# Moving output projections, product order and vector sums in three groups of a fused attention and MLP kernel

## Chip, cores, metric

One core of a Trainium2 chip. The metric is the device time of one execution in microseconds (us); the median over executions is quoted with its range. The profiler's span of an execution is some 1.8 us shorter than its time.

## The reference, cut to what matters

```python
x = A_x                                            # 1 x 2048 x 576, bf16
h = x + A(layernorm(x), A_wqkv, A_wo)              # dilated sliding-window attention, then "@ wo"
h2 = h + B(layernorm(h), B_w1, B_b1, B_w2, B_b2)   # MLP: gelu(y @ w1 + b1) @ w2 + b2, hidden width 4608
```

## The kernel before

The 16 tiles of 128 tokens are done in eight groups of two. A group has MLP1 (its results in PSUM go through gelu on ScalarE), the output projection `@ wo` of the next group's two tiles, LayerNorm of those, and MLP2. So a group's projections start the chain that ends with the next group's normalized, transposed rows.

From group 3 on, MLP2 multiplies part of its 18 pairs of row blocks in 2x2 blocks with seven products instead of eight. Each "product" n is a run of matmuls that add into one PSUM bank, and their left and right sides are partly sums made by VectorE. Pairs beyond `rows` (8, 12, 12, 16, 18, 18 in groups 3 to 8) are done in the plain way. One product's result starts several outputs: ScalarE copies it ("seeds") from one bank into another, `b` from the first product's bank into the sixth's, `d` from the sixth's into the fifth's, `f` from the fifth's into the third's.

```python
bank = {1: a, 2: a, 3: f, 4: b, 6: b}          # 7 and 5: banks of the projections' PSUM tiles, free after "h"
seed = {"b": (1, 6), "d": (6, 5), "f": (5, 3)}
if SR < rows < NM:        # group 6
    steps = [(1, all_), "b", "wo", "h", "e", (2, all_), "11", (6, lo), (7, lo), "6", "7", (6, hi), "d", (7, hi), "rest", "in",
             (5, all_), "f", "exp", (4, all_), "21", "22", "o1", "4", (3, all_), "12", "o0", "3"]
elif rows <= SR:          # groups 3 to 5
    steps = [(1, all_), "b", "wo", "h", "e", (2, all_), "11", (6, all_), "d", "6", "7", (7, all_), "rest", "in", ...]
elif not last:            # group 7
    steps = [(1, lo), "wo", (1, hi), "b", "h", "e", (7, lo), (6, all_), "d", "6", "7", (2, all_), (7, hi), "rest", "in", ...]
...                       # cut: group 8
```

An entry like `(6, lo)` is product 6 over the first 12 pairs of row blocks (`hi`: the rest, `all_`: both), "wo" the projections, "11" and its like plain rows. "h", "6", "7", "in" are hooks: what VectorE, ScalarE and the queues get at that point of their own orders. In "h" are the residual adds (`ln2_h`, which read the projections' PSUM tiles and so free them), LayerNorm's statistics (`ln2_act`, ScalarE) and sums for the products; in "6" and "7" LayerNorm's applies (`ln2_send`).

```python
def ln2_h(j):                                   # residual add on VectorE
    pw = pw_of.pop(j)
    h = sb.tile([P, D], F32, tag="h", name="h", bufs=2)
    nc.vector.tensor_tensor(out=h[:]..., in0=pw[:, :, 0:HALF], in1=x_of(j)..., op=ALU.add)

def phase(duo, swap, after):                    # MLP1 and the projections: pairs of 64-row matmuls
    ... nc.tensor.matmul(duo["g"][r ^ swap][i], lhsT=lhsT, rhs=rhs, ...)   # lhsT, rhs: 64 partitions
```

## Time and profile before

| | us |
|---|---|
| median of the first three runs | 365.69 (365.05 to 365.73) |
| span of the profiled run | 363.3 |
| group 5, MLP1's end to MLP2's end | 18.69 |
| group 6 | 18.65 |
| group 7 | 17.96 |

TensorE's order is fixed, so the stretch from the end of a group's last MLP1 matmul to the end of its last MLP2 matmul, read from TensorE's timeline, repeats within 0.02 us where nothing waits. Whole executions scatter by half a microsecond or more.

The following line is of TensorE's timeline (start, length, engine, line, operation, count), just before the wait for the seed copy that the prediction shows at 283.34.

```profile
282.65 0.41 PE L667 MATMUL po<-w2b_sb,h_all 128*128 128x288 f16 x2
```

Two matmuls are recorded with 0.41 us, 0.286 for the last, but matmuls follow each other every 0.1226. The next could have started at 282.65 + 2 x 0.1226 = 282.90, and it started at 283.34. So 0.44 us is lost. Lost time is read from starts.

### The profile page before, as it was taken

How to read it: one execution, taken by the hardware profiler on the slowest of the kernel's cores; microseconds unless marked ns; L12 is line 12 of the kernel's file. 1: busy time of each engine (PE TensorE's matmuls, PEld its weight loads, DVE VectorE, ACT ScalarE, POOL GpSimd, SP SyncE). 2: the span in 40 equal slices, each digit the busy share in tenths (PEclk: the TensorE clock that was granted, in tenths of full speed). 3: DMA queues.
4: the chain of work that ended last, by engine and by line, in shares of the span. 5: the costliest groups of instructions: out<-in, count | busy, mean ns of one | idle time of the engine just before them, and what ended most of it. 6: DMA issues, size and time to landing. Idle time of an engine off the chain costs nothing.

```text
span 363.3 us, 11427 instructions
## 1 busy us (share of the span) xinstructions
PE 357.6 (98%) x4895; PEld 290.5 (80%) x4895; DVE 300.6 (83%) x426; ACT 228.9 (63%) x507; POOL 39.4 (11%) x47
## 2 busy tenths in 40 slices
PE   8999999999999999999999999999999999999996
PEld 4688877888788877887788778877887788778874
DVE  5999999999999999999999899979998498720431
ACT  4779856799526763668556855685568656615630
POOL 2251004000120030103100211020101010100000
PEclk9999999999999999999999999999999999999999
DMA  7989899964445733720552145304530352030001
GB/s 235 299 204 306 223 260 236 363 219 78 145 89 107 218 111 87 152 40 34 137 106 71 35 125 115 72 32 109 118 71 33 74 102 56 3 89 19 2 2 33
DMA packets 61908, 43.70 MB, mean 120 GB/s; under 512 B 31889, under 2 KB 60177, under 8 KB 61857
## 3 DMA queue, kind: packets, MB, share of 16 engines
q1 hardware_dynamic: 59968, 41.13, 41.1%
q0 software_dynamic: 1728, 1.77, 4.8%
q8 instruction: 38, 0.62, 0.7%
q10 hardware_dynamic: 160, 0.07, 0.1%
q14 instruction: 14, 0.11, 0.1%
HBM read 21.10 MB, written 12.42 MB: 92 GB/s over the span
## 4 chain that ended last, share of the span: by engine, by line
PE 94%; DMA 2%; ACT 1%; SPq 1%; DVE 0%; issue 0%
PE pm L217 39%; PE po L667 25%; PE pq L217 14%; PE po L579 10%; PE pw L217 5%; DMA wq_sb<-in_A_wqkv_dram 1%; SPq L104 1%; PE xt_pt L182 1%; DMA x_all<-b_bc 1%; ACT hn L175 0%; ACT hn L479 0%; PE h_pt L182 0%; PE o_pt L182 0%; DVE h L461 0%; ACT hn L478 0%
## 5 line engine op out<-in xcount | busy, mean ns | idle before, releaser
L560 ACT ACTIVATE h_all<-pm,b_sb 128x256 f16<-128x256 f32 (+1 forms) x288 | 108.3, 496 | 74.3 <-PE pm L217 74.3
L217 PE MATMUL pm<-hnT,w_sb 64*128 64x256 bf16 x2304 | 143.0, 269 | 0.0
L217 PEld LDWEIGHTS <-w_sb 64*128 64x128 bf16 x2304 | 111.6, 94 | 15.1 <-issue 1.7
L667 PEld LDWEIGHTS <-h_all 128*128 128x128 f16 x528 | 50.8, 98 | 14.9 <-issue 2.5
L217 PE MATMUL pq<-wq_sb,xnT 64*128 64x288 bf16 x768 | 54.5, 283 | 0.8 <-DMA wq_sb<-in_A_wqkv_dram 0.7
L217 PEld LDWEIGHTS <-xnT 64*128 64x128 bf16 x864 | 42.4, 94 | 11.3 <-issue 1.1
L351 DVE TENSOR_TENSOR prod<-prod 128x2304 bf16<-128x2304 bf16 (+1 forms) x64 | 44.2, 691 | 2.1
L667 PE MATMUL po<-w2a_sb,h_all 128*128 128x288 bf16 (+1 forms) x302 | 42.0, 286 | 0.0
L397 DVE TENSOR_TENSOR prod<-kv_ring,probs 128x4608 bf16<-128x4608 bf16 x16 | 40.9, 2554 | 0.8 <-DMA kv_ring<-kv_dram 0.5
L345 DVE TENSOR_TENSOR prod<-kv_ring,q_all 128x4608 bf16<-128x4608 bf16 x16 | 40.8, 2549 | 0.2
L217 PE MATMUL pm<-hnT,w1h_sb 64*128 64x256 bf16 x288 | 39.2, 269 | 0.0
L403 DVE TENSOR_TENSOR prod<-prod 128x2304 bf16<-128x2304 bf16 (+1 forms) x32 | 33.8, 1057 | 1.0
L579 PEld LDWEIGHTS <-h_all 128*128 128x128 bf16 x288 | 27.8, 98 | 7.9 <-issue 1.0
L481 POOL TENSOR_TENSOR ln_rstd<-ln_var,mhalf 128x1 f32<-128x1 f32 x13 | 14.5, 1115 | 175.1 <-ACT ln_var L480 175.1
L667 PEld LDWEIGHTS <-kv_ring 128*128 128x128 f16 x240 | 23.5, 98 | 6.4 <-issue 0.5
L579 PE MATMUL po<-w2a_sb,h_all 128*128 128x288 bf16 x224 | 28.5, 286 | 0.0
L647 DVE TENSOR_TENSOR kv_ring<-h_all 128x1536 f16<-128x1536 f16 (+3 forms) x10 | 6.9, 687 | 17.3 <-ACT h_all L560 17.3
L667 PE MATMUL po<-w2b_sb,h_all 128*128 128x288 bf16 (+1 forms) x142 | 21.2, 286 | 0.0
L217 PE MATMUL pw<-wo_sb,oT 64*128 64x288 bf16 x256 | 19.5, 283 | 0.0
L162 POOL TENSOR_TENSOR ln_rstd<-ln_veps,mhalf 128x1 f32<-128x1 f32 (+2 forms) x14 | 13.3, 954 | 48.2 <-DVE ln_veps L156 31.8
L217 PEld LDWEIGHTS <-oT 64*128 64x128 bf16 x288 | 13.5, 94 | 4.8 <-issue 1.7
L739 ACT COPY po<-po 128x288 f32<-128x288 f32 x18 | 6.9, 384 | 16.2 <-PE po L667 13.0
(117 smaller groups left out, 383.1 us busy)
## 6 DMA issues: line engine op xcount, KB each, us to landing
w_sb<-in_B_w_dram SPq DMA_DIRECT2D x6, 768.0 KB, 5.5
kv_ring<-kv_dram SPq DMA_DIRECT2D x28, 144.0 KB, 2.6
w2a_sb<-in_B_w_dram SPq DMA_DIRECT2D x4, 1008.0 KB, 6.6
kv_dram<-kv_ring SPq DMA_DIRECT2D x13, 288.0 KB, 3.3
out_dram<-o_sb SPq DMA_DIRECT2D x15, 144.0 KB, 2.5
td<-q_all SPq DMA_DIRECT2D x14, 144.0 KB, 2.2
td<-hn SPq DMA_DIRECT2D x14, 144.0 KB, 1.8
x_all<-in_A_x_dram SPq DMA_DIRECT2D x12, 144.0 KB, 2.9
```

The lines of the kernel that those rows point to most:

```text
L162: nc.gpsimd.tensor_tensor(out=rstd[:], in0=veps[:], in1=mhalf[:].to_broadcast([P, n]), op=ALU.pow)
L217: last = nc.tensor.matmul(duo["g"][r ^ swap][i], lhsT=lhsT, rhs=rhs, start=(swap == 0 and i == 0 and kt == 0), stop=(swap == 1 and kt == K ...
L345: nc.vector.tensor_tensor(out=prod[:], in0=k_ring[j % 2], in1=q_all[:, j, :].unsqueeze(1) .to_broadcast([P, W, D]), op=ALU.mult)
L351: nc.vector.tensor_tensor(out=prod[:, :, o * H:o * H + n], in0=prod[:, :, a * H:a * H + n], in1=prod[:, :, c * H:c * H + n], op=ALU.add)
L397: nc.vector.tensor_tensor(out=prod[:].rearrange("p w (d h) -> p w d h", h=H), in0=v_ring[j % 2].rearrange("p w (d h) -> p w d h", h=H), in ...
L403: nc.vector.tensor_tensor(out=prod[:, 0:n, :], in0=prod[:, 0:n, :], in1=prod[:, n:2 * n, :], op=ALU.add)
L481: nc.gpsimd.tensor_tensor(out=rstd[:], in0=var[:], in1=mhalf[:], op=ALU.pow)
L560: pace[0] = nc.scalar.activation(out=hT(grp)[:, f, 0:N], in_=ps[:, r, i * N:(i + 1) * N], func=ACT.Gelu_apprx_tanh, bias=b1_sb[:, f:f + 1] ...
L579: nc.tensor.matmul(banks[half], lhsT=hT(grp)[:, f, i * P:(i + 1) * P], rhs=w2_rows(f)[:, half * HALF:(half + 1) * HALF], start=(f == 0), s ...
L647: nc.vector.tensor_tensor(out=s_slot(t, m0, m1), in0=a, in1=b, op=alu)
L667: nc.tensor.matmul(bank, lhsT=l, rhs=r, start=start, stop=stop, skip_group_check=True)
L739: nc.scalar.copy(out=bank[seed[step][1]], in_=bank[seed[step][0]])
```

## The change

In groups 5 to 7 the projections are issued first, directly behind MLP1; in groups 5 and 6 the seventh product's first rows come between the first and second product (in group 7 they lay there already), and plain rows (in 6 also the seventh product's last rows) lie between the sixth and the fifth, which waits for the sixth's seed copy. The first residual add and LayerNorm's first statistics get a hook of their own ("hc") ahead of the first seed copy. In group 6 the seventh product's sum, and in group 7 the sums of rows 12 to 17, go behind the residual adds. The intent is a TensorE without gaps. Cut to its core:

```diff
-        if SR < rows < NM:
-            steps = [(1, all_), "b", "wo", "h", "e", (2, all_), "11", (6, lo), (7, lo), "6", "7", (6, hi), "d", (7, hi), "rest", "in",
-        ...
+        if rows < NM:
+            steps = [(1, all_), "b", "wo", "hc", "h", "e", (2, all_), "11", (6, all_), "d", "6", "7", (7, all_), "rest"] if not first_wo \
+                else ["wo", "hc", (1, all_), "b", "h", "e", (7, lo), (2, all_), (6, all_), "6", "d", "rest", "7", "11"] if rows == SR \
+                else ["wo", "hc", (1, all_), "b", "h", "e", (7, lo), (2, all_), (6, all_), "6", "7", "d", "11", (7, hi), "rest"]
+            steps += ["in", (5, all_), "f", "exp", (4, all_), "21", "22", "o1", "4", (3, all_), "12", "o0", "3"]
         elif not last:
-            steps = [(1, lo), "wo", (1, hi), "b", "h", "e", (7, lo), (6, all_), "d", "6", "7", (2, all_), (7, hi), "rest", "in",
+            steps = ["wo", "hc", (1, all_), "b", "h", "e", (7, lo), (6, all_), "6", "d", "7", (2, all_), (7, hi), "rest", "in",
 ...
-                early = {2: (), 3: (0,)}.get(k, (0, 2))
+                early = {2: (), 4: (0, 2)}.get(k, (0,))
 ...
+                if k == 5:                                             # k counts groups from 0
+                    x["h"] += [c_(h_sums, 0, SR, (2,)), c_(h_sums, 0, SR, (1, 3))]
 ...                                                                    # group 7: sums of rows 12 to 17 behind the adds
-                    x["h"] = [c_(ln2_stats, c, d)] + x["h"]
+                    x["hc"] = [c_(ln2_h, c), c_(ln2_act, c)] + x["hc"]
+                    x["h"] = [c_(ln2_h, d), c_(ln2_act, d), c_(put_b2, c), c_(put_b2, d)] + x["h"]
 ...
-            mlp2_fast(g, rows, (p, q, r, s), wo, x)
-            p, q, r, s = r, s, p, q
+            if 4 <= k < 7:
+                mlp2_fast(g, rows, (s, p, q, r), wo, x, True)          # other PSUM tiles for the projections
+                p, q, r, s = q, r, p, s
+            else:
+                mlp2_fast(g, rows, (q, p, r, s), wo, x)
+                p, q, r, s = r, s, p, q
```

More of the change, by code (lines that the diff above doesn't have):

```diff
@@ L683, in halves, with mlp2_fast @@
         return ap.rearrange("p (g c) -> p g c", g=2)
-    def mlp2_fast(g, rows, tags, wo, hooks):
-        p, q, r, s = tags
+    def mlp2_fast(g, rows, tags, wo, hooks, first_wo=False):
         last = wo is None
+        q, p, r, s = tags
         j0, j1 = g
@@ L722, in mlp2_fast @@
         }
-        if SR < rows < NM:
-            steps = [(1, all_), "b", "wo", "h", "e", (2, all_), "11", (6, lo), (7, lo), "6", "7", (6, hi), "d", (7, hi), "rest", "in",
-                     (5, all_), "f", "exp", (4, all_), "21", "22", "o1", "4", (3, all_), "12", "o0", "3"]
-        elif rows <= SR:
-            steps = [(1, all_), "b", "wo", "h", "e", (2, all_), "11", (6, all_), "d", "6", "7", (7, all_), "rest", "in",
-                     (5, all_), "f", "exp", (4, all_), "21", "22", "o1", "4", (3, all_), "12", "o0", "3"]
+        if rows < NM:
[3 more added lines that the diff above has]
+            steps += ["in", (5, all_), "f", "exp", (4, all_), "21", "22", "o1", "4", (3, all_), "12", "o0", "3"]
         elif not last:
-            steps = [(1, lo), "wo", (1, hi), "b", "h", "e", (7, lo), (6, all_), "d", "6", "7", (2, all_), (7, hi), "rest", "in",
+            steps = ["wo", "hc", (1, all_), "b", "h", "e", (7, lo), (6, all_), "6", "d", "7", (2, all_), (7, hi), "rest", "in",
                      (5, all_), "f", (4, all_), "o1", (3, all_), "o0"]
@@ L1015 @@
             home = k % 2
-            x = {n: [] for n in ("h", "6", "7", "in", "exp", "4", "3")}
+            x = {n: [] for n in ("hc", "h", "6", "7", "in", "exp", "4", "3")}
             if k < 6:
@@ L1025 @@
                     m1[3] += [c_(w2_sums, 0, 8)]
-                early = {2: (), 3: (0,)}.get(k, (0, 2))
+                early = {2: (), 4: (0, 2)}.get(k, (0,))
                 m1[3] += [c_(h_sums, 0, min(rows, SR), early)]
-                x["h"] += [c_(h_sums, 0, min(rows, SR), [t for t in range(4) if t not in early])]
+                if k == 5:
+                    x["h"] += [c_(h_sums, 0, SR, (2,)), c_(h_sums, 0, SR, (1, 3))]
+                else:
+                    x["h"] += [c_(h_sums, 0, rows, [t for t in range(4) if t not in early])]
                 if k == 5:
@@ L1040 @@
                 m1[3] = [c_(h_sums, 0, SR)]
-                mid[3] = {1: [c_(h_sums, SR, 16)]}
-                x["h"] += [c_(h_sums, 16, NM)]
+                if k == 7:
+                    mid[3] = {1: [c_(h_sums, SR, 16)]}
+                    x["h"] += [c_(h_sums, 16, NM)]
             if k + 3 < len(GROUPS):
@@ L1048 @@
                 if k == 6:
-                    x["h"] = [c_(ln2_h, c), c_(ln2_act, c), c_(ln2_h, d)] + x["h"] \
-                        + [c_(ln2_more, d), c_(ln2_rstd, d), c_(ln2_send, c), c_(add_b2, c), c_(add_b2, d), c_(ln2_bias, d)]
+                    x["hc"] += [c_(ln2_h, c), c_(ln2_act, c)]
+                    x["h"] += [c_(ln2_h, d), c_(ln2_more, d), c_(ln2_rstd, d), c_(h_sums, SR, NM), c_(ln2_send, c),
+                               c_(ln2_bias, d), c_(add_b2, c), c_(add_b2, d)]
                     x["6"] += [c_(ln2_hn, d), c_(ln2_out, d)]
                 else:
-                    x["h"] = [c_(ln2_stats, c, d)] + x["h"]
+                    x["hc"] = [c_(ln2_h, c), c_(ln2_act, c)] + x["hc"]
+                    x["h"] = [c_(ln2_h, d), c_(ln2_act, d), c_(put_b2, c), c_(put_b2, d)] + x["h"]
                     x["6"] += [c_(ln2_send, c)]
@@ L1058 @@
             mlp1(g, mlp1_plan(p, q, r, s, (r, s, p)), m1, mid)
-            mlp2_fast(g, rows, (p, q, r, s), wo, x)
-            p, q, r, s = r, s, p, q
+            if 4 <= k < 7:
+                mlp2_fast(g, rows, (s, p, q, r), wo, x, True)
+                p, q, r, s = q, r, p, s
+            else:
+                mlp2_fast(g, rows, (q, p, r, s), wo, x)
+                p, q, r, s = r, s, p, q
 _INS = ['A_x', 'A_wqkv', 'A_wo', 'B_x', 'B_w1', 'B_b1', 'B_w2', 'B_b2']
```

## The prediction

> **What bounds the kernel now.** I read the page first (shares of the engines, granted clock), then the chain of waits in order of time, then TensorE's waits, then the timelines around the three places that the change touches. From the page:
>
> ```profile
> PE 357.6 (98%) x4895; PEld 290.5 (80%) x4895; DVE 300.6 (83%) x426; ACT 228.9 (63%) x507; POOL 39.4 (11%) x47
> ...
> PEclk9999999999999999999999999999999999999999
> ```
>
> TensorE (PE) is busy 357.6 of 363.3 us at full clock, so no other engine's time can buy more than the little in which TensorE stands. Its end times are modelled, though, so I count instructions in the chain (start, length, engine, tile, count):
>
> ```profile
> 124.51 2.21 PE pw L217 x36
> 126.71 17.75 PE po L579 x144
> ...
> 217.92 17.79 PE pm L217 x324
> 235.71 1.58 PE po L667 x12
> 237.29 2.31 PE pw L217 x36
> 239.60 14.81 PE po L667 x120
> 254.41 17.79 PE pm L217 x324
> 272.20 2.07 PE po L667 x16
> ...
> 282.99 0.30 ACT po L739
> ...
> 283.34 7.51 PE po L667 x60
> 290.85 17.79 PE pm L217 x324
> 308.64 1.58 PE po L667 x12
> 310.22 2.31 PE pw L217 x36
> 312.53 14.07 PE po L667 x114
> 326.60 17.79 PE pm L217 x324
> ```
>
> Here pm is MLP1, pw the attention's output projection, po MLP2. MLP1 and the projections are 64-row matmuls in pairs, MLP2 uses all 128 rows. Groups 5, 6 and 7 have their MLP1 start at 217.92, 254.41 and 290.85. The reader is to see two things. First, the rate: a group's 120 MLP2 matmuls take 14.81 us, 36 projection matmuls in group 2 (124.51) take 2.21, that is 18 pairs of 0.123. Second, the corners: where projections follow MLP1 directly (group 2) they take 2.21; where they follow a piece of MLP2, 2.31. Twelve MLP2 matmuls after MLP1 take 1.58 instead of 12 x 0.1226 = 1.47. So each change between 64 and 128 rows costs about 0.10 to 0.11 us.
>
> The waits of TensorE after 120 us are a single line, and the timeline has its place, group 6:
>
> ```profile
> PE po L667 <- ACT po L739: 0.3, 1, 0.3
> ...
> 282.12 0.87 ACT L175 ACTIVATE hn<-h,ln_nmean,ln_rstd 128x576 bf16<-128x576 f32 x1
> 282.90 0.39 ACT L739 COPY po<-po 128x288 f32<-128x288 f32 x1
> 283.34 1.63 PE L667 MATMUL po<-x_all,kv_ring 128*128 128x288 f16 x12 [0.29 <-ACT po L739]
> ```
>
> The seed copy from the sixth product's bank into the fifth's stands behind LayerNorm's work on ScalarE (ACT), and TensorE waits for it.
>
> **What the Trainium skill says.** "TensorEngine Tiling (Array Packing)", section Key Properties: a change of tiling mode, not just of tile, drains TensorE. The trace agrees and gives the size, 0.10 to 0.11 us. "TensorE: Matmul & The Clock Gate", section Part 2 (what happens when you issue a matmul): matmuls stay in program order and only weight loads are pulled ahead. So a projection put first that must wait holds up all behind it. "Perfetto Trace Analysis", section on the Tensor Engine instruction, says that TensorE's end times are estimated, which is why I used starts and counts.
>
> **The change part by part.** No row count changes, so the number of matmuls, vector sums and activations is the same. Groups 1 to 4 and 8 keep their order (the new hook is only a split of the old list, and the tag names are swapped twice). What moves is in groups 5, 6 and 7.
>
> 1. Projections next to MLP1. Before: pm, po, pw, po, pm: four changes of mode. After: pm, pw, po, pm: two. Saved per group: 0.11 (po after pm) + 0.10 (pw after po) = 0.21. Check on whole groups: group 2 from 124.51 to 144.46 is 19.95 us for 162 matmul times, 162 x 0.1226 = 19.86, so 0.09 over. Group 5 from 235.71 to 254.41 is 18.70 for 12 + 18 + 120 = 150, 18.39, so 0.31 over. The difference is 0.22. Three groups: 3 x 0.21 = 0.63 us.
>
> 2. Group 6's stall. From 272.20 to 290.85 are 18.65 us for 16 + 18 + 112 = 146 matmul times, 17.90, plus 0.31 for the changes: 18.21. So 0.44 is lost, of which 0.29 shows as a wait and the rest, I estimate, as a refill. In the new order the projections end about 2 us earlier, so LayerNorm's activations do too, and the plain rows (4 matmuls, 0.49 us) and the seventh product's last 4 (0.49) lie between sixth and fifth. With MLP1's end as zero: ScalarE's last gelus end at 2.78 (270.50 + 4.48 - 272.20), LayerNorm's two statistics at 1.9 each (276.92 to 278.83 before), with the first seed copy between, run to about 7, its two applies at 1.1 each (281.81 to 282.90) to about 9.1. The sixth product ends at 2.31 + (16 + 12 + 16 + 16) x 0.1226 = 9.7, with step 3's wait 9.9, and the copy near 10.3; the fifth starts near 10.8. The 0.44 goes.
>
> 3. A new small wait in group 6. VectorE (DVE) is late there: its first sum runs from 273.24 to 274.19, or 1.99 after MLP1. Then come the two residual adds, 1.34 together (276.13 to 277.47 before), to 3.33, and then the seventh product's sum, 0.95, to about 4.3. TensorE reaches the seventh product at 2.21 + 0.10 + 16 x 0.1226 = 4.27. With the signal's way I charge 0.2 us. In group 5 both early sums are done at 1.5, in group 7 at 0: nothing there.
>
> 4. Groups 5 and 7 elsewhere. Group 5: the sixth product ends at 2.31 + 48 x 0.1226 = 8.2, ScalarE has by then made both statistics and one apply (2.8 + 1.9 + 0.4 + 1.8 + 1.1 = 8.0), and the copy runs to about 8.6; 12 plain matmuls (1.47) lie before the fifth product, which starts near 9.7: 1.1 us to spare. Group 7: after the first sums VectorE does two residual adds (1.4), statistics (1.2) and four sums of rows 12 to 17 (about 1.9), from 1.9 to about 6.3; the sixth product needs the second of them near 7.4. It fits.
>
> Sum: 0.63 + 0.44 - 0.20 = 0.87 us. From the median 365.69 that is 364.82; from the mean of the three runs, 365.49, it is 364.62. I take 364.8.
>
> **The rivals.**
>
> Projections wait at the front. They need two PSUM tiles and two transposed attention tiles. The second tile is the one whose gelus are first of MLP1's last twelve: in group 5 they end about at 234.01 + 4 x 0.373 = 235.5, before MLP1's 235.71, and it is used 0.6 later. Group 2 has that very order and its projections take 2.21: against a stall. The attention tile is nearer the edge in group 7:
>
> ```profile
> 305.87 1.21 SPq L433 DMA_TRANSPOSE oT<-td  x1
> ...
> DMA to landing us min/median/max: 2.8/2.9/2.9
> ```
>
> It lands near 308.75. Before, it was wanted after 310.8; now at 308.64 + 0.61 = 309.25. Half a microsecond is left; if the store before it lands later, TensorE waits the difference. I give it one in five, some 0.3 us. It would make the time 365.1.
>
> Residual adds ahead of the sums make the sums late, and the sixth product waits in groups 5 to 7. For it: VectorE is 83% busy overall and nearly full through group 5. Against it: it sat idle 1.94 us in group 5 and 0.94 in group 6 waiting for the projections, which now come as much earlier. If it held, 0.3 to 0.8 us a group, and the time would be 365 to 366.5.
>
> The changes of mode are only moved, or the drain is hidden already: then only group 6's 0.44 is left, less 0.2, and the time is 365.5. Group 2's row speaks against it.
>
> Engines off the path gain and the kernel with them: VectorE's idle time shrinks, but TensorE's matmuls end the time, so it is worth nothing. A gain over 2%, 7.3 us, has nothing to come from: all that TensorE loses in these groups is 1.4 us.
>
> **Range and chances.** The steps give 0.2 (all goes to new waits) to 1.2 us (no new wait and a little more). The three runs of before spread over 0.7 us, so a median may be off by some 0.3. Range 364.1 to 365.8. Faster by over 2%: 0.01. Within 2%: 0.98. Slower by over 2%: 0.01, for a wait that I have overlooked, which would have to be over 2 us in each group.
>
> **What would show it.** Step 1: the chain should have 2.21 for the projections right after MLP1 in groups 5 to 7, and one MLP2 piece after them; group 5 from MLP1's end to the next MLP1 18.5 us, group 7 17.75. Step 2: no wait of TensorE for the seed copy; group 6 in 18.0 to 18.2 instead of 18.65. Step 3: a wait of 0.1 to 0.2 for a vector sum before the seventh product in group 6 alone. Wrong would be: a projection that waits for the transposed tile or for a gelu, a wait for sums in groups 5 or 7, a clock under full speed, or MLP1 of the next group held up by its normalized rows.

## The result, and the profile after

The changed kernel took 364.31 us (363.95 to 364.97, six runs), before in the same rounds 365.12 (364.93 to 365.73, six runs). The ratio is 0.9976, 95% interval 0.9962 to 0.9990.

The chain of the changed kernel in order of time (start, length, engine, tile, count), from group 5 on:

```profile
235.98 2.21 PE pw L217 x36
238.19 16.27 PE po L667 x132
254.46 17.79 PE pm L217 x324
272.25 2.21 PE pw L217 x36
274.46 15.92 PE po L667 x128
290.38 17.79 PE pm L217 x324
308.17 2.21 PE pw L217 x36
310.37 15.54 PE po L667 x126
```

In each of the three groups there is now one piece of projections (pw), at 2.21 instead of 2.31, and one of MLP2 (po). ScalarE's copy and the detour through LayerNorm have left the chain. From MLP1's end to MLP2's end the groups take 18.48, 18.12 and 17.75 us: 0.21, 0.53 and 0.21 less, together 0.95. The span fell by only 0.7 (363.3 to 362.6), since group 1's MLP1 ended 0.26 later in this execution, in work that the change does not touch.

All waits of TensorE in that execution (engine, tile and line, releaser: us, times, longest):

```profile
PE pq L217 <- DMA wq_sb<-in_A_wqkv_dram: 1.0, 3, 0.5
PE busy L782 <- PEq L1084: 0.8, 1, 0.8
```

Both are from the warm-up and the QKV stage ahead of group 1, so none is left in MLP2. Yet group 6 has a small loss that shows only in the starts. TensorE's and VectorE's timelines there:

```profile
276.12 0.41 PE L667 MATMUL po<-w2b_sb,h_all 128*128 128x288 bf16 x2
276.48 3.36 PE L667 MATMUL po<-w2a_sb,h_all 128*128 128x288 f16 x26
...
275.48 0.95 DVE L647 TENSOR_TENSOR h_all<-h_all 128x1536 f16<-128x1536 f16 x1
```

The seventh product could have started at 276.12 + 0.245 = 276.37; it started at 276.48, 0.05 after VectorE's (DVE) sum for it ended at 276.43. That is 0.11 us.

### The profile page after: what moved, and what is told of

Its sections match the earlier page's. It is cut to its first block, busy times and chain, and to the rows that moved or that the text cites. A ratio compares the mean times of both kernels' runs of the same rounds, so it can differ in the third digit from the quotient of the medians. Undisturbed runs are those within 1.5% of the kernel's fastest.

```text
span 362.6 us, 11419 instructions
## 1 busy us (share of the span) xinstructions
PE 357.3 (99%) x4895; PEld 290.9 (80%) x4895; DVE 300.3 (83%) x422; ACT 228.9 (63%) x507; POOL 39.3 (11%) x47
## 4 chain that ended last, share of the span: by engine, by line
PE 96%; DMA 1%; SPq 1%; DVE 0%; issue 0%
PE pm L217 39%; PE po L667 27%; PE pq L217 14%; PE po L579 10%; PE pw L217 5%; DMA wq_sb<-in_A_wqkv_dram 1%; SPq L104 1%; PE xt_pt L182 1%; PE o_pt L182 0%; PE h_pt L182 0%; PE xt_pt L186 0%; DVE o_sb L698 0%; PE h_pt L186 0%; PE o_pt L186 0%; PE xt_pt L184 0%
## 5 line engine op out<-in xcount | busy, mean ns | idle before, releaser
L647 DVE TENSOR_TENSOR kv_ring<-h_all 128x1536 f16<-128x1536 f16 (+4 forms) x9 | 6.7, 745 | 16.0 <-ACT h_all L560 16.0
```

Of the source, the lines that this page charges most:

```text
L647: nc.vector.tensor_tensor(out=s_slot(t, m0, m1), in0=a, in1=b, op=alu)
```

## The experiments

Besides the kernel before, twelve kernels ran, all correct, the changed one twice. The table has each one's lengths from MLP1's end to MLP2's end, in us, and its median time; the two with small matmuls have longer groups by design, and their times are of two executions each.

| kernel | group 3 | 4 | 5 | 6 | 7 | time | ratio to before |
|---|---|---|---|---|---|---|---|
| before | 19.18 | 18.70 | 18.69 | 18.65 | 17.96 | 365.12 to 365.40 | |
| changed | 19.19 | 18.69 | 18.48 | 18.12 | 17.75 | 364.31 | 0.9976 |
| changed, again | 19.18 | 18.69 | 18.48 | 18.88 | 17.75 | 364.38 | 0.9978 |
| projections behind | 19.18 | 18.69 | 19.98 | 20.17 | 19.70 | 369.84 | 1.0119 |
| projections only | 19.19 | 18.69 | 19.16 | 18.81 | 17.74 | 366.38 | 1.0027 |
| seed copy first | 19.51 | 18.69 | 18.70 | 18.34 | 17.95 | 369.35 | 1.0094 |
| third sum first | 19.18 | 18.69 | 18.48 | 18.42 | 17.75 | 364.54 | 0.9974 |
| second product first | 19.19 | 18.69 | 19.89 | 19.20 | 17.75 | 366.35 | 1.0035 |
| statistics behind | 19.19 | 18.70 | 19.49 | 18.57 | 17.75 | 365.81 | 1.0014 |
| sums first | 19.18 | 18.69 | 18.94 | 22.40 | 19.02 | 370.56 | 1.0141 |
| small 64-row matmuls | 20.93 | 21.30 | 21.09 | 23.07 | 24.36 | 389.03 | 1.0649 |
| small 128-row matmuls | 19.39 | 19.00 | 18.79 | 18.55 | 18.21 | 366.48 | 1.0032 |
| projections first in 3 to 7 | 23.75 | 20.38 | 18.48 | 18.41 | 17.75 | 371.20 | 1.0158 |
| sums later | 19.19 | 18.69 | 18.48 | 17.99 | 17.75 | 364.13 | 0.9968 |

### The cost of a change of row mode by itself

Both runs are the changed kernel with one tiny matmul, into an unused half of a PSUM tile, behind each matmul of the fourth product. They differ in its rows alone.

```diff
+                for m in range(*step[1]):
+                    mm(b, h_block(1, 1, m, m + 1), t_slot(3, m, m + 1), False, m == step[1][1] - 1)
+                    nc.tensor.matmul(spare, lhsT=ident[sl, :], rhs=ident[sl, 0:16], start=True, stop=True, skip_group_check=True)
# sl = 0:64 in the first run, 0:128 in the second
```

> The disputed cost by itself: the changed kernel with one small 64-row matmul (16 columns, into an unused half of a PSUM tile) behind each of the fourth product's 84 matmuls in groups 3 to 8, so 168 more changes of row mode. To be read against the next run, where the same small matmul has 128 rows. Theory (a change of mode costs 0.10 to 0.11 us each): 84 x 0.21 = 17.6 us more than with 128 rows. Rival (it is a cost of the first matmul on other data, or hidden by the next weights' load): the two within 2 us.

> As the run before with 128 rows, so no change of mode. Theory: each small matmul costs its own weight load, some 0.05 to 0.1 us, 4 to 8 us in all over the changed kernel. With the run of 64 rows 17.6 us above it, if a change of mode costs what the corners of the trace say.

TensorE's timeline in group 4, first with 64 rows:

```profile
212.79 0.30 PE L667 MATMUL po<-kv_ring,h_all 128*128 128x288 f16 x1
...
213.13 0.30 PE L667 MATMUL po<-kv_ring,h_all 128*128 128x288 f16 x1
```

and with 128 rows:

```profile
211.12 0.28 PE L667 MATMUL po<-kv_ring,h_all 128*128 128x288 f16 x1
...
211.27 0.28 PE L667 MATMUL po<-kv_ring,h_all 128*128 128x288 f16 x1
```

A large matmul and its small neighbour take 0.34 us when the mode changes and 0.15 when it does not. By the groups: (20.93 - 19.39) / 8 in group 3, (21.30 - 19.00) / 12 in group 4 and (21.09 - 18.79) / 12 in group 5 are each 0.192 us for two changes, so 0.096 a change in the mean. The small matmul itself costs 0.026 ((19.00 - 18.69) / 12), less than the expected 0.05. The rival, a cost that is hidden anyway, falls. What the cost consists of, these runs do not separate. TensorE's weight loads give a hint: the small matmul's own load (0.09 us) starts with it at 212.68 where the mode changes, and at 211.13, 0.12 ahead of its matmul at 211.25, where it doesn't. So the 0.096 may be a weight load that is no longer made ahead.

The whole difference is 22.6 us, not 17.6. In groups 6 to 8 the granted clock fell below full speed (mean 0.93 in group 6's stretch and 0.87 in group 7's), though TensorE stood recorded as busy all the time; with 128 rows it was 1.00 in both stretches. In group 6 it was 0.50 from 297.0 to 300.0 and 1.00 before. Only the groups at full clock measure the change of mode.

### One part undone: projections behind the first product

```diff
-                else ["wo", "hc", (1, all_), "b", "h", "e", (7, lo), ...
+                else [(1, all_), "wo", "hc", "b", "h", "e", (7, lo), ...      # in groups 5, 6 and 7; PSUM tiles as before
```

> The changed kernel with one part undone: in groups 5 to 7 the projections stand behind the first product again. Theory (the gain is four changes of row mode made two, and the early seventh product only works because the projections are early): each of the three groups gains 0.21 us for two more changes, and the seventh product now comes too soon. Group 5 waits about 0.2 us for a PSUM tile of the projections, group 6 about 1.8 us for the third vector sum, which stands behind the residual adds, group 7 about 0.3. From MLP1's end to the next MLP1: group 5 18.9, group 6 20.2, group 7 18.3 us; the kernel some 2.9 us slower than the change, 2 us slower than before. Rival (the gain comes from the order of the products, the place of the projections is indifferent): groups 18.5, 18.1 and 17.7 as in the change.

TensorE's timeline has a new wait in group 5:

```profile
242.42 1.63 PE L667 MATMUL po<-w2a_sb,h_all 128*128 128x288 bf16 x12 [0.70 <-ACT po L738]
```

The rival falls: the three groups grow by 1.50, 2.05 and 1.95 us. Group 6's 20.17 and its wait of 1.90 for the third sum are as expected. Groups 5 and 7 were expected at 18.9 and 18.3. Their waits for the residual adds are 0.36 each, but after the seventh product comes one of 0.70 for the first seed copy in each, which I had not counted, and in group 7 one of 0.29 for the last gelus. This was the first sign that the seed copy `b` matters.

### One part done alone: projections first

```diff
+        if first_wo:                     # groups 5 to 7 of the kernel before; PSUM tiles as in the change
+            steps.remove("wo")
+            steps = ["wo"] + steps
```

> The kernel before with one part done: in groups 5 to 7 the projections go first, nothing else moves. Theory: groups 5 and 7 come down from 18.70 and 17.96 to 18.48 and 17.74 us, as in the change. In group 6 the seed copy still stands on ScalarE behind LayerNorm, whose first statistics stand behind the other seed copy, which waits for the first product; about 0.35 us of the stall stays, so group 6 takes 18.4 to 18.5 instead of 18.65 (18.13 in the change). In all 0.65 us under before. Rival A (changes of mode cost nothing, the stall was all): groups 5 and 7 as before. Rival B (early projections alone heal the stall): group 6 18.0 to 18.1.

Group 7 is as expected (17.74), so rival A falls. In that group the seventh product follows the first already in the kernel before. Group 5 is not: 19.16 instead of 18.48. It did not gain 0.21 but lost 0.47. TensorE and ScalarE (ACT) there:

```profile
239.63 0.38 ACT L742 COPY po<-po 128x288 f32<-128x288 f32 x1 [1.07 <-issue]
...
240.06 2.12 PE L667 MATMUL po<-w2a_sb,h_all 128*128 128x288 bf16 x16 [0.52 <-ACT po L742]
```

The second product adds to bank `a`, and the copy reads the first product's result from that bank. So the second must wait until the copy has read. In the kernel before, the projections lay between the two and covered the copy. Moved to the front they bare it: 0.52 us of wait, 0.68 with what the records hide. Group 6 pays the same (a second wait of 0.52) and keeps part of its old one (the fifth product starts at 284.01 instead of 283.87, 0.14). So rival B falls too. The old stall shrank from 0.44 to 0.14 us, partly because TensorE itself now comes later, but the new wait costs more, and the time was 366.38, if anything over that of before (interval of the ratio 0.9998 to 1.0057).

### One part undone: the second product ahead of the seventh

```diff
-                else ["wo", "hc", (1, all_), "b", "h", "e", (7, lo), (2, all_), (6, all_), ...
+                else ["wo", "hc", (1, all_), "b", "h", "e", (2, all_), (7, lo), (6, all_), ...   # groups 5 and 6
```

> The changed kernel with one part undone: in groups 5 and 6 the seventh product stands behind the second again, in group 7 nothing changes. Theory now (the second product adds to the bank that ScalarE's first seed copy is reading, so TensorE must wait for that copy unless other work lies between; the projections did that before, the seventh product does it after the change): a wait for the seed copy between first and second product of about 1.25 us in group 5 and 0.9 in group 6; group 5 19.7, group 6 18.9, group 7 17.75. Rival (the seventh product's place is indifferent, as my prediction took it): 18.48 and 18.0 to 18.1.

TensorE and ScalarE in group 5:

```profile
241.10 0.39 ACT L738 COPY po<-po 128x288 f32<-128x288 f32 x1
...
241.54 1.63 PE L667 MATMUL po<-w2a_sb,h_all 128*128 128x288 bf16 x12 [1.25 <-ACT po L738]
```

A wait of 1.25 us in group 5 and 1.05 in group 6 for that copy, as the theory had it, and 19.89 and 19.20 us. The seventh product between first and second is what covers the first seed copy once the projections are gone from there.

### One part undone: LayerNorm's first statistics behind the first seed copy

```diff
-                else ["wo", "hc", (1, all_), "b", "h", ...
+                else ["wo", (1, all_), "b", "hc", "h", ...           # groups 5 to 7; changes ScalarE's order alone
```

> The changed kernel with one move on ScalarE undone: in groups 5 to 7 LayerNorm's first statistics stand behind the first seed copy, as before; TensorE's and VectorE's orders stay. Theory: the seventh product hides the copy in both orders, so group 5 keeps 18.48 and group 7 17.75; in group 6 LayerNorm's work then ends about 1 us later and the copy into the fifth's bank comes about 0.4 us late: 18.5 to 18.6 instead of 18.12. Rival (ScalarE's order is indifferent once the projections come first): 18.12 in group 6.

Group 6 (18.57) and group 7 (17.75) are as expected. Group 5 lost 1.01 us, where I expected nothing. GpSimd (POOL), VectorE and TensorE there:

```profile
242.31 2.62 POOL L481 TENSOR_TENSOR ln_rstd<-ln_var,mhalf 128x1 f32<-128x1 f32 x1 [22.76 <-ACT ln_var L480]
...
241.95 2.55 DVE L345 TENSOR_TENSOR prod<-kv_ring,q_all 128x4608 bf16<-128x4608 bf16 x1
...
246.50 1.63 PE L667 MATMUL po<-x_all,kv_ring 128*128 128x288 f16 x12 [0.85 <-ACT po L738]
```

LayerNorm's first `pow` on one column took 2.62 us; in the changed kernel's group 5 it took 0.63. Started 1.5 us later, it fell beside VectorE's long product, and ended 0.43 after it. The apply waits for it (ScalarE stood 0.91), the copy `d` stands behind the apply, and the fifth product waits. The Trainium skill, "GPSIMD Engine Reference", section Specifications, says that GpSimd's SBUF interfaces are shared with VectorE and contend with its instructions of two SBUF inputs; the trace agrees in this place, 2.62 us against 0.63. It is no exception: the second `pow` of the changed kernel's group 5 started beside that product too (243.03) and took 1.87 us, to 0.41 after the product's end.

### One part undone: residual adds behind the sums

```diff
+                if 4 <= k < 6:
+                    n = len(x["hc"]) + 4
+                    h = x["hc"] + x["h"]
+                    x["hc"], x["h"] = [], h[n:n + 3] + h[:n] + h[n + 3:]
+                elif k == 6:
+                    h = x["h"]
+                    x["h"], x["hc"] = [h[3]] + x["hc"] + h[:3] + h[4:], []
```

> The changed kernel with one part undone: in groups 5 to 7 the residual adds stand behind the vector sums again. Theory (the residual adds must go first, since they free the PSUM tile that the seventh product takes, and start LayerNorm): TensorE waits before the seventh product in group 5 about 0.4 us, group 6 about 2.7, group 7 about 1.2; some 4 us slower than the change. Rival (the order on VectorE is of no account, since TensorE is the bound): within 0.3 us of the change.

TensorE in group 6:

```profile
279.96 4.85 PE L667 MATMUL po<-w2a_sb,h_all 128*128 128x288 f16 x26 [2.73 <-DVE h L461]
```

The rival falls. TensorE waits for a residual add 0.31, 2.73 and 1.11 us in the three groups. Groups 5 and 7 grow by 0.46 and 1.27 as expected; group 6 by 4.28 instead of 2.7, since behind the long wait the granted clock was 0.50 from 280.0 to 283.0. The edit does one thing more than its heading says: it puts LayerNorm's first statistics behind the first seed copy too, as in the run before. The waits for the residual adds are read directly, so the reading does not rest on the times alone.

### ScalarE's order alone, in the kernel before

```diff
-  (6, lo), (7, lo), "6", "7", (6, hi), "d", (7, hi), "rest", "in",
+  (6, lo), (7, lo), (6, hi), "d", "6", "7", (7, hi), "rest", "in",     # group 6
```

> The kernel before with one move on ScalarE: in group 6 the seed copy from the sixth product's bank to the fifth's is issued ahead of LayerNorm's two applies. Theory (the stall is a matter of ScalarE's order alone): group 6 falls from 18.65 to 18.25 to 18.35 us, the wait of TensorE for the copy goes or falls under 0.1, groups 5 and 7 stay at 18.70 and 17.96. Rival (the stall needs the projections earlier): group 6 stays near 18.65.

Group 6 fell to 18.34 and TensorE's wait for the copy went, as expected. And yet the kernel was 4.0 us slower. The queue's and TensorE's timelines, then two stretches (us, then busy time of TensorE, of its weight loads, VectorE, ScalarE and GpSimd, granted clock, DMA share, GB/s):

```profile
289.05 2.53 SPq L496 DMA_TRANSPOSE hnT<-td  x2
...
293.35 0.89 PE L217 MATMUL pm<-hnT,w_sb 64*128 64x256 bf16 x8 [2.58 <-DVE prod L397]
```

```profile
290.70:293.35 2.65, 0.07 (x2) 0.03 (x2) 2.65 (x3) 0.00 (x0) 0.00 (x0) 1.00 0.69 162
293.35:297.00 3.65, 3.65 (x38) 3.22 (x40) 3.55 (x5) 0.00 (x0) 1.78 (x2) 0.53 0.72 129
```

The applies now stand behind the copy, and the rows for the next group's MLP1 come too late: their transposes started at 289.05 instead of 285.01, the second one landed near 293.2, and MLP1 of group 7 began at 293.35. The profile names VectorE as the releaser, but before that same matmul began 0.08 us ahead of that same product, so it does not depend on it; that it was the transposed rows is inferred from their landing. After 2.6 us of standing the clock was granted at 0.53 for 3.65 us: MLP1 of group 7 ended 22.12 us after MLP2 of group 6 instead of 17.79, 4.33 more: 2.59 of standing and 1.74 of slow clock. The slow clock is not certain to follow: one of this kernel's four executions had a mean clock of 1.000 and took 367.53 us, the others 0.995 and 369.3 to 369.6. Why group 3, which this kernel does not touch, was 0.33 longer here: VectorE reached the residual add 0.69 later than in the kernel before (166.18 against 165.49). It was that late already at group 2's residual adds (128.19 against 127.50), behind waits of 1.21, 0.34 and 0.23 us for transfers into the attention's ring, where the kernel before has one of 0.5.

### The change once more

> The changed kernel once more, beside the next run on one chip. Theory: 0.7 to 1.0 us under before (ratio 0.9973 to 0.998), groups 5 to 7 at 18.48, 18.13 and 17.74 us from MLP1's end to the next MLP1. A rival of chance (the 0.8 us between the medians is scatter of the start): the groups' lengths stay but the times of before and after overlap.

The ratio is 0.9978 (0.9963 to 0.9994), so the gain stands. But the run that was profiled was the slowest of six (365.57), and its group 6 took 18.88. VectorE and TensorE:

```profile
259.49 2.56 DVE L397 TENSOR_TENSOR prod<-kv_ring,probs 128x4608 bf16<-128x4608 bf16 x1 [0.77 <-DMA kv_ring<-kv_dram]
...
276.67 0.95 DVE L647 TENSOR_TENSOR h_all<-h_all 128x1536 f16<-128x1536 f16 x1
...
277.68 3.36 PE L667 MATMUL po<-w2a_sb,h_all 128*128 128x288 f16 x26 [0.71 <-DVE h_all L647]
```

A transfer into the ring came late by 0.77 us. VectorE is full in this stretch and carries the delay for 17 us to the sum ahead of the seventh product. So the 0.11 us of the first profile is what is lost when no transfer is late.

### Group 6's third sum ahead of the residual adds

```diff
-                early = {2: (), 4: (0, 2)}.get(k, (0,))
+                early = {2: (), 4: (0, 2), 5: (0, 2)}.get(k, (0,))
-                    x["h"] += [c_(h_sums, 0, SR, (2,)), c_(h_sums, 0, SR, (1, 3))]
+                    x["h"] += [c_(h_sums, 0, SR, (1, 3))]
```

> The changed kernel with one VectorE operation moved: in group 6 the seventh product's sum goes ahead of the residual adds again. Theory (the 0.115 us gap before the seventh product in group 6 is the wait for that sum, and LayerNorm can bear 0.9 us of delay): the gap goes, group 6 takes 18.00 to 18.05 instead of 18.13, groups 5 and 7 unchanged; 0.1 us in all. Rival (the gap is the PSUM tile which the first residual add frees, or the delay of LayerNorm brings back the seed stall): group 6 18.2 to 18.6.

The gap before the seventh product went, but group 6 took 18.42: now the second product waits 0.27 us for the first seed copy, as ScalarE's first statistics start 0.9 later. The rival was right that the delay of LayerNorm's work brings a stall back, and wrong about which: it is the copy `b`.

### Two tries to beat both

The first is the run above with projections first in groups 3 and 4 too:

```diff
+                else ["wo", "hc", (1, all_), "b", "h", "e", (2, all_), "11", (6, all_), "d", "6", "7", (7, all_), "rest"] if g in GROUPS[2:4] \
-            if 4 <= k < 7:
+            if 2 <= k < 7:
```

> A version meant to beat both: projections first in groups 3 and 4 too (their other order unchanged), and the third sum ahead of the residual adds in group 6. Theory: groups 3 and 4 fall by 0.21 us each (19.18 to 18.97, 18.70 to 18.48), group 6 by 0.11; 0.5 us under the change, 1.4 under before. Rival (VectorE is too far behind in these groups, so that early projections wait or hold PSUM tiles, which is why the change left them out): groups 3 and 4 get a new wait and stay or grow.

The rival holds. Groups 3 and 4 grow by 4.57 and 1.68 us over the kernel before. In group 3:

```profile
167.94 0.39 ACT L739 COPY po<-po 128x288 f32<-128x288 f32 x1
...
168.38 4.22 PE L667 MATMUL po<-w2a_sb,h_all 128*128 128x288 bf16 x20 [3.01 <-ACT po L739]
```

VectorE reaches the first residual add at 165.25 there, the statistics follow, the copy `b` follows them, and no seventh product covers it. Only about 3.2 of the 4.57 us are that wait; behind it the granted clock was 0.50 from 168.38 to 171.00. In group 4, behind a wait of 1.74, it stayed at 1.00.

The second try moves VectorE's work in group 6 of the changed kernel:

```diff
+                early = {2: (), 4: (0, 2), 5: (0, 2)}.get(k, (0,))
-                    m1[1] += [c_(w2_sums, 12, 14)]
-                    x["h"] += [c_(h_sums, SR, rows), c_(w2_sums, 14, 16)]
+                    x["h"] += [c_(w2_sums, 12, 14, (0, 1)), c_(w2_sums, 14, 16, (0, 1)), c_(h_sums, SR, rows)]
+                    x["h"] += [c_(w2_sums, *ms, (t,)) for t in (2, 3) for ms in ((12, 14), (14, 16))]
```

> A version meant to beat both: the changed kernel, only VectorE in group 6 reordered. The four weight sums of rows 12 and 13 (1.7 us) move from MLP1 to behind the first twelve rows' sums, so that both early sums end near 1.2 us after MLP1 and the residual adds find the projections' PSUM tiles at once. Theory (the gap before the seventh product in group 6 is VectorE's lateness, and the run with 0.7 us of it differs by one late transfer): group 6 takes 18.00 to 18.05 us, no wait for a sum, also where a transfer is late; 0.1 us under the change, 1.1 under before. Rival (the moved sums are late for the sixth product or the last rows of the seventh): a new wait in group 6 of 0.3 us or more.

Group 6 took 17.99 us, and its profile has no wait of TensorE after 100 us. The time was 364.13 (363.80 to 364.46, five runs), ratio to before 0.9968 (0.9954 to 0.9982). By the clock it cannot be told from the change, whose intervals overlap it, and no late transfer fell into its profile; the trace shows 0.13 us less in group 6. It is the best kernel by that measure.

## Why the prediction was right, point by point

- **Step 1, projections next to MLP1 (0.63).** Right. The chain has 2.21 three times; groups 5 and 7 fell by 0.21 each. The small matmuls measure 0.096 us a change apart from the corners. But the sum assumed that a place on TensorE can be left without cost. It cannot: projections alone made group 5 longer by 0.47.
- **Step 2, group 6's stall (0.44).** Right in the sum, too simple in the cause. The prediction let the 0.44 go because LayerNorm's activations end earlier with the projections. The runs show that three things are needed: projections early, the first statistics ahead of the first seed copy (without it 0.45 us more in group 6, 1.01 in group 5) and the seventh product over that copy (without it 1.08 more in group 6, 1.41 in group 5). That the second product must wait for the first copy is in no line of the prediction; its trace of before hid it under the projections. The changed kernel happened to bring the cover that the prediction did not know to be needed; so far its figure was luck. And the rest of the 0.44 beside the printed 0.29 was no refill, as it estimated, but the recorded length of a matmul that hides 0.163 us of any gap.
- **Step 3, a new wait in group 6 (0.20).** Right: 0.11 us in the first profile, 0.87 in the second, where a transfer was late. The cause is the one named, VectorE's sum, as the two kernels that move this sum ahead show (0.00 left before the seventh product, by starts).
- **Step 4, groups 5 and 7 elsewhere.** Right. Group 5's 1.1 us to spare measured 0.89 (the copy ended at 244.59, the fifth product started at 245.48): the run with the statistics behind used it up.
- **Sum.** Predicted 0.87 us; the three groups gave 0.95, the medians 0.81. Predicted time 364.8, measured 364.31, inside the range; most of the difference is the kernel before, 365.12 in these rounds and not 365.69.
- **Rivals.** The transposed tile of group 7 was issued 3.3 us ahead of the projections (304.85 against 308.17), and they did not wait. The sums behind the residual adds cost only the 0.11 of step 3; the other order costs 4.28 in group 6, of which, as an estimate, 1.5 are clock (half of the 3 us at 0.50). That a piece put first which must wait holds up all behind it, as the prediction said, shows where projections alone moved: the second product's wait made the whole of group 5 0.47 longer. The changes of mode are not hidden.

What stays open is how often a late transfer costs group 6 its 0.9 us. One of two profiles of the changed kernel shows it, and that one was taken of the slowest of its six runs. In the nine profiles of its variants VectorE waited for that same transfer twice more, 0.31 and 0.33 us.

## What to carry to other kernels

When TensorE is 98% busy, what is left to win are corners: count its instructions between two marks and compare with the steady rate, for short gaps are not printed as waits. Before moving work on the bound engine, ask what that work was covering: here the projections hid a copy out of a PSUM bank, and the move paid only together with another product put in their place. And a reordering on a helper engine is to be followed to the next stage: the seed copy put first cured one stall of 0.4 us and made one of 2.6, or 4.3 with the slow clock behind it, by delaying the next group's input.

## What the Trainium skill lacked or had wrong

- "TensorEngine Tiling (Array Packing)", section Key Properties, says that a change of tiling mode drains TensorE, and gives no size. Here it is 0.096 us a change between 64 and 128 rows, in a stream of 128x288 matmuls at full clock, and the 64-row weights behind a change began to load with their matmul (both at 212.68), not ahead of it.
- "Perfetto Trace Analysis", section on the Tensor Engine instruction, says that TensorE's end times are estimated, and not what follows for gaps. Here a 128x288 matmul is recorded with 0.286 us at a spacing of 0.1226, so the first 0.163 us of any gap is not printed.
- "TensorE: Matmul & The Clock Gate", Part 1, puts the fall to the low clock after at least one idle window of about 3.4 us. Here 2.65 us with almost no matmul (290.70 to 293.35) was enough: the granted clock was 0.53 for the next 3.65 us, in this execution. Waits of 2.73 and 3.01 us were followed by the same fall in the profiles, waits of 1.74 and 1.90 were not. And rapid changes of mode with no idle time in the records (which hide gaps under 0.163 us) lowered the mean clock of a stretch to 0.93 and 0.87, against 1.00 without changes of mode; the page's section on a second HAM failure mode tells of short idle times between groups of matmuls, not of changes of mode.
